# Moving some twenty entries of the order tables of an attention loop by one or two steps

## The chip, the cores and the metric

The kernel runs on one core of one Trainium2 chip. The metric is the device time of one execution in microseconds; the median of three runs is taken. Smaller is better.

## What is computed

The input x has 2048 tokens of 512 numbers in f32. Four residual layers follow one another, A, B, A, B, with the same weights for both A and both B. Each has 32 heads of 16.

```python
x = x + A(layernorm(x)); x = x + B(layernorm(x)); x = x + A(layernorm(x)); x = x + B(layernorm(x))
# A: linear attention, phi = concat(softmax(p), softmax(-p)) with p = head @ w_phi
kv, z = einsum(phi_k, v), sum(phi_k)
o = (phi_q @ kv) / (phi_q @ z + 1e-6)          # then o @ wo
# B: four segments s of 512 tokens, memory M, z carried from one to the next
a_dot = softmax(q_s k_s^T / 4 + causal mask) @ v_s
a_mem = (phi(q_s) @ M) / (phi(q_s) @ z + 1e-6)  # phi(t) = t + 1 or exp(t)
o_s = g * a_mem + (1 - g) * a_dot               # g = sigmoid(beta), then o @ wo
M, z = M + phi(k_s)^T v_s, z + sum(phi(k_s))
```

## The kernel before

**Order.** The program lists the instructions of every engine in the order in which they run. A helper chains each instruction to the one before it on its engine, so no engine takes a later one first: L208 records the matmuls, L212 the transposes on TensorE, and L186 everything on VectorE, ACT, GpSimd (POOL) and the DMA issues of SyncE (SP). That is why almost every row of the profile carries one of these three lines, and rows are told apart by the names of what they write and read. What an engine does next is therefore set by the tables below, and an instruction that waits holds everything behind it on its engine.

**Layer A** (`LayerA`, L653) has a first pass of feature steps for keys, values and queries, and a second pass for the products. In the first pass, run once at 33 to 174 us and once at 697 to 851 us, the table VALUES (L80) gives the step at which each of the quarters of the next segment's value projection is issued. Its first row is used once, for the first segment of the second A layer; the second row is used five times.

**Layer B** (`LayerB`, L1030) is run by `steps` (L1498), at 238 to 709 us and 915 to 1382 us. It has 160 steps, numbered k, 40 for each segment s; within a segment they are written m.j, with m from 0 to 7 (half of a group of eight heads) and j from 0 to 4. Each step does, in this order:

- `attend` (L1282): TensorE writes logits of scores into the PSUM tile lg (one buffer of two banks), ACT takes the exponential into P, POOL clears the masked half (affine_select);
- `maxima` (L1240), for the half nine steps ahead: TensorE writes logits into the tiles mx and my (one bank each), VectorE takes masked maxima from them into mxs, in two instructions of 128×512 or in four shorter ones;
- memory work that is due (POOL, SP, ACT), and then two lists of what was put off: `later` and `late`, with `weighted` (L1323, the product of P with v into the one bank pv, which ACT empties) between them; then the norm pieces that were put off as `rows`;
- the words of the table's cell for this step (`do`, L1510).

**The words.** q, k, v and out issue quarters of a projection or of the output, as many as stand behind the slash; a quarter is 6 matmuls on 64-row weights (tiles w, oh, ol) or 3 matmuls of 128×512 (wqk, hh, hl), and when a tile of 128 tokens is complete, its PSUM banks are emptied. These banks come from one pool, g, of three. A plus takes the next segment's projection. max is a transpose of the maxima into g, an ACT copy (mt) and a DMA. t0 to t3 are four transposes of one block of the keys' features into g and an ACT copy. x0 to x3 load a tile of the residual into xr (three buffers) with a DMA on SP, L1438. a and m read and update the memory, pre loads such a tile for the early part of the last output (tb), p its quarters, ln and n advance the normalization of a coming segment; an n is put into `rows`, so it runs in the next step, and depending on how far the norm is it issues a load of x on SP, or statistics, or an ACT normalization.

**The tilde.** Behind a word it sets `put_off` (L160, L163, L1511), and then the instruction that empties the last bank isn't issued in this step but appended to `late`:

```python
def wait(f):
    if put_off[0] is None:
        f()
    else:
        put_off[0].append(f)
```

For out that is the whole end of a tile (`end` in L1443): one addition on VectorE for each of its one or two PSUM banks, into xr, and the store of xr on SP. For a projection it is the subtraction on VectorE that leaves the low part.

**Tables.** FIRST (L86) orders segment 0, GAPS (L96) segments 1 and 2, LAST (L107) segment 3 of the first B layer and FINAL (L117) that of the second. BEFORE (L127) holds the steps ahead of k = 0. So an entry of GAPS is used four times, one of BEFORE twice, one of LAST or FINAL once.

Of the kernel before, what the change touches and what calls it, by code (L numbers as in the profile page):

```python
# [76 lines left out]
OUTROWS = ((), (1, 2, 3), (1, 2, 3), (1, 2, 3))  # L77
VROWS = ((3,), (0, 1, 2, 3), (0, 1, 2, 3), (0, 1, 2, 3))
ROWS = ((0, 2, 3, 4, 4, 8, 9, 11, 13), (4, 7, 9, 15))
VALUES = ((11, 12, 14, 15, 17, 19, 20, 22, 24, 25, 26, 27, 30, 32, 33, 35), (10, 11, 13, 14, 16, 18, 19, 21, 23, 24, 26, 27, 29, 31, 32, 34))  # L80
NORMS = (14, 20, 21, 21, 22, 23, 24, 27, 29, 31, 33)
OPENING = (0, 0, 1, 0, 1, 0, 1, 1, 1, 1, 0, 1, 1, 1, 1, 1, 1, 1, 1)

# [14 lines left out]
1.0 m0 n n q3/1 | 1.1 q3/2 | 1.2 n max q3/1~ | 1.3 t1 k3/2 | 1.4 k3/2~  # L98
2.1 max out/2 | 2.2 m1 | 2.3 ln ln out/1 | 2.4 a2 ln~ x0
3.1 max ln out/1~ | 3.2 x1 | 3.3 t2 q0+/4 | 3.4 out/3  # L100
4.0 out/1 x2 | 4.1 k0+/4~ max load | 4.3 out/2 | 4.4 n a3 out/2
5.0 t3 x3 m2 q1+/1 | 5.1 max q1+/2 | 5.2 q1+/1 | 5.3 out/2 n | 5.4 out/2
6.0 k1+/1 | 6.1 max k1+/3 | 6.2 m3 | 6.3 v0+/4 | 6.4 n a0+ v1+/2
7.0 n | 7.1 v1+/2 max begin | 7.2 n | 7.3 t0+ q2+/4~ n N | 7.4 v2+/4~ N
"""

LAST = """  # L107
0.1 max k2/4~ | 0.2 n | 0.3 v3/2 n | 0.4 a1 n v3/2~ n
1.0 n | 1.1 q3/3 max | 1.2 q3/1~ n | 1.3 k3/2 n | 1.4 k3/2~ n
2.1 max out/1 | 2.3 out/2 | 2.4 a2 x0 pre ln~  # L110
3.1 ln max ln~ | 3.3 x1 pre out/1 ln~ | 3.4 out/3
4.1 max | 4.2 out/1 | 4.3 pre out/3 x2 | 4.4 a3 out/1 v/2 x3
5.0 v/2 | 5.1 out/4 | 5.2 max | 5.3 fin v/2 | 5.4 v/2 pre
6.1 v/2 max | 6.3 v/2 fin | 6.4 v/2
7.1 pt v/2 p/3 | 7.2 v/2 | 7.3 fin v/2 p/3 | 7.4 p/3
"""
# [2 lines left out]
1.1 max q3/3 | 1.3 q3/1 | 1.4 k3/2  # L119
2.1 max k3/1 | 2.3 k3/1 out/1 pre | 2.4 a2 x0  # L120
3.1 max x1 out/2 | 3.3 out/1 pre | 3.4 out/2
4.1 out/2 | 4.2 max pre | 4.3 out/2 x2 | 4.4 a3 out/2
5.1 x3 out/2 | 5.2 max | 5.3 out/2 | 5.4 fin pre
6.1 max | 6.3 fin
7.0 pt | 7.1 p/2 | 7.3 p/3~ | 7.4 fin p/4
"""
BEFORE = {-25: 'v0 q0 load', -20: 'k0', -17: 'n', -16: 'n v1 n', -15: 'n n', -14: 'q1 n', -13: 'n', -12: 'k1 n n', -8: 'n v2', -6: 'q2~', -4: 't0', -3: 'max'}  # L127


@with_exitstack  # L130
def interleave_kernel(ctx, tc, x_in, a_wqkv, a_wphi, a_wo, b_wq, b_wk, b_wv, b_wo, b_beta,
# [416 lines left out]
    def v_tile(hT, w, vv, tag, order=range(4), paired=False, rows=()):  # L548

        v = sp.tile([P, 4, VROW], F32, tag="v", bufs=2, name=nm("v"))  # L550
        vv[:] = [v]
        if paired:
            for j in (0, 2 * VW - 1):
                pool.memset(v[:, :, 0 : H * VW].rearrange("p t (h e) -> p t h e", e=2 * VW)[:, :, :, j : j + 1], 1.0)
            pool.memset(v[:, :, H * VW : H * VW + 1], 1.0)
            shape = dict(e=2 * VW), slice(1, 2 * VW - 1), dict(e=2 * DH)
        else:
            pool.memset(v[:, :, 0 : H * VW].rearrange("p t (h e) -> p t h e", e=VW)[:, :, :, DH : DH + 1], 1.0)
            pool.memset(v[:, :, H * VW : VROW], 0.0)
            shape = dict(e=VW), slice(0, DH), dict(e=DH)  # L560
        for n, t in enumerate(order):
            vt = v[:, t, 0 : H * VW].rearrange("p (h e) -> p h e", **shape[0])[:, :, shape[1]]
            if n in rows:
                po = [PS(*tag) for _ in range(2)]
                yield from halves(po, lambda a, kc: hT[a][:, kc, t * P : (t + 1) * P], lambda b, kc: w[b][:, kc, :])
                act.copy(vt, po[0].rearrange("p (h e) -> p h e", **shape[2]))
                wait(lambda vt=vt, p=po[1]: dve.tensor_tensor(out=vt, in0=p.rearrange("p (h e) -> p h e", **shape[2]), in1=vt, op=ADD))
            else:
                po = PS(*tag)
                yield from tok_proj(po, hT, t, w)  # L570
                act.copy(vt, po.rearrange("p (h e) -> p h e", **shape[2]))
            yield
# [80 lines left out]
    class LayerA:  # L653
# [88 lines left out]
        def pass1(self, first):  # L742
# [35 lines left out]
            for n, s in enumerate(SEGS):  # L778
# [51 lines left out]
                if n < NSEG - 1:  # L830
                    hTs, g = upc
                    vv = []
                    plan = [(j, g) for j in ROWS[0 if n == 0 and not first else 1]]
                    vals, norms = VALUES[0 if n == 0 and not first else 1], NORMS
                    vt = v_tile(hTs, wv, vv, ("g", G))
# [194 lines left out]
    class LayerB:  # L1030
# [467 lines left out]
        def steps(self, side, after, table_end):  # L1498
# [71 lines left out]

            table = {k: (v.split(), 0) for k, v in BEFORE.items()}
            memory = {"a": {}, "m": {}}
# [122 lines left out]
```

## Time and profile before

| | |
|---|---|
| median of 3 runs | 1381.26 us (1380.68 to 1382.15) |
| profiled execution | 1383.75 us, its span 1382.0 us |
| granted TensorE clock | 0.998 |
| ACT: busy, instructions | 814.8 us, 1244 |
| GpSimd: busy, instructions | 735.5 us, 1073 |
| DMA | 225.35 MB, 163 GB/s on average |

A row of the timeline gives start and length in us, engine, line, operation, the tile written, the tiles read, shape, and how many such instructions follow in a row; in brackets stands how long the engine sat idle before it, and what ended this. A row of the waits gives engine, tile and line, what it waited for, and then the total, the number of times and the longest. Matmul lengths overlap, so what a matmul costs TensorE is read from the distance between starts. A row of the chain has start, length, engine or DMA, and tile.

### The profile page before, as it was taken

To read this page: it belongs to the slowest core of one execution; us is meant where nothing else is said; L and a number is where in the kernel's file an instruction comes from. 1 tells how busy PE (TensorE), PEld (TensorE's weight loads), DVE (VectorE), ACT (ScalarE), POOL (GpSimd) and SP (SyncE) were. 2 spreads that over 40 slices of the span, in tenths; PEclk is the share of its full clock that TensorE was granted. 3 is DMA by queue.
4 is the path that set the end of the run, shared out by engine and by line. 5 is a ranking of instruction groups with operands and counts; after the bars stand their busy time and mean duration, and the time that the engine had idled before them with its cause. 6 is when DMAs were issued, how large, how long until landed. Compare 5 with 4: busy or idle time off the path is not lost.

```text
span 1382.0 us, 34402 instructions
## 1 busy us (share of the span) xinstructions
PE 1353.2 (98%) x12598; PEld 962.1 (70%) x12598; DVE 986.8 (71%) x3074; ACT 814.8 (59%) x1244; POOL 735.5 (53%) x1073
## 2 busy tenths in 40 slices
PE   9999999999999999999999999999999999999998
PEld 8887878775666666665568887887656666666564
DVE  5766888587667667777547768958776776676774
ACT  5555445447686676666544434553676866866653
POOL 1678855224656666554534346642356656745543
PEclk9999999999999999999999999999999999999999
DMA  6369285546666647658541103855465666566552
GB/s 202 121 217 332 103 278 181 178 137 185 173 146 196 182 121 195 179 152 214 173 144 37 62 32 113 282 167 166 140 194 138 168 176 186 152 173 160 145 149 72
DMA packets 135735, 225.35 MB, mean 163 GB/s; under 512 B 21328, under 2 KB 39888, under 8 KB 135568
## 3 DMA queue, kind: packets, MB, share of 16 engines
q1 hardware_dynamic: 134464, 222.91, 55.7%
q8 instruction: 101, 1.65, 0.5%
q14 instruction: 66, 0.54, 0.1%
q10 hardware_dynamic: 1104, 0.24, 0.1%
HBM read 116.39 MB, written 43.25 MB: 116 GB/s over the span
## 4 chain that ended last, share of the span: by engine, by line
PE 84%; DVE 6%; DMA 3%; ACT 2%; issue 2%; POOL 2%; SPq 0%; POOLq 0%; DVEq 0%; ACTq 0%
PE g L208 51%; PE pv L208 11%; PE lg L208 8%; PE mx L208 5%; PE g L212 4%; PE my L208 3%; PE lg L212 2%; ACT P L186 1%; DVE junk L186 1%; PE pv L212 1%; DVE es L186 1%; POOL P L186 1%; DVE xr L186 1%; DVE ta L186 1%; DVE my L186 1%
## 5 line engine op out<-in xcount | busy, mean ns | idle before, releaser
L186 ACT ACTIVATE P<-lg 128x1024 f32<-128x1024 f32 x316 | 324.8, 1028 | 149.8 <-PE lg L208 128.4
L186 POOL TENSOR_SCALAR_AFFINE_SELECT P<-P 128x256 f32<-128x256 f32 (+1 forms) x448 | 190.6, 441 | 356.7 <-ACT P L186 350.2
L186 DVE CUSTOM_DVE_ANT_0 junk<-mx,mask 128x128 uint8<-128x128 f32 (+2 forms) x384 | 146.6, 420 | 88.5 <-PE my L208 54.4
L208 PE MATMUL g<-hh,wqk 128*128 128x512 f32 x512 | 187.3, 413 | 0.8 <-DMA wqk<-wqk 0.8
L208 PE MATMUL g<-w,oh 128*128 128x512 f32 (+1 forms) x652 | 172.9, 414 | 0.0
L208 PE MATMUL lg<-e,e 64*128 64x512 f32 (+1 forms) x1010 | 163.1, 373 | 4.7 <-ACT P L186 4.1
L208 PE MATMUL pv<-P,v 128*32 128x512 f32 (+3 forms) x2048 | 166.5, 441 | 0.1
L208 PE MATMUL g<-w,hh 64*128 64x512 f32 (+1 forms) x656 | 152.4, 407 | 2.9 <-ACT mmq L186 1.5
L208 PE MATMUL my<-e,e 63*128 63x256 f32 (+3 forms) x519 | 147.8, 345 | 4.8 <-DVE mxs L186 4.3
L208 PE MATMUL mx<-e,e 63*128 63x256 f32 (+3 forms) x519 | 147.6, 336 | 2.8 <-DVE mxs L186 2.8
L186 DVE CUSTOM_DVE_ANT_0 junk<-my,mask 128x128 uint8<-128x128 f32 (+2 forms) x384 | 146.9, 420 | 0.1
L208 PEld LDWEIGHTS lg<-e,e 64*128 64x128 f32 x1010 | 87.2, 185 | 84.2 <-issue 33.9
L186 DVE CUSTOM_DVE_ANT_0 mx<-mx,mask 128x512 f32<-128x512 f32 x128 | 89.0, 695 | 57.9 <-PE my L208 37.4
L208 PEld LDWEIGHTS pv<-P,v 128*32 128x32 f32 x2048 | 53.6, 109 | 101.2 <-issue 90.1
L208 PEld LDWEIGHTS g<-hh,wqk 128*128 128x128 f32 x512 | 96.3, 188 | 29.9 <-issue 9.2
L208 PEld LDWEIGHTS g<-w,oh 128*128 128x128 f32 (+1 forms) x652 | 93.8, 188 | 21.5 <-issue 9.1
L208 PE MATMUL g<-w,ol 128*128 128x512 f32 (+1 forms) x326 | 104.8, 396 | 1.6 <-DVE ol L186 1.6
L208 PEld LDWEIGHTS g<-w,hh 64*128 64x128 f32 (+1 forms) x656 | 89.5, 186 | 23.4 <-issue 4.3
L186 DVE DVE_READ_ACCUMULATOR2_ANT mxs<- 128x1 f32 x1024 | 101.0, 99 | 0.0
L208 PE MATMUL g<-hl,wqk 128*128 128x512 f32 x256 | 100.4, 392 | 0.0
L208 PEld LDWEIGHTS mx<-e,e 63*128 63x128 f32 (+1 forms) x519 | 91.7, 186 | 12.1 <-issue 4.5
L208 PEld LDWEIGHTS my<-e,e 63*128 63x128 f32 (+1 forms) x519 | 85.7, 186 | 17.7 <-DVE mxs L186 7.2
(191 smaller groups left out, 2897.3 us busy)
## 6 DMA issues: line engine op xcount, KB each, us to landing
e<-ta SPq DMA_DIRECT2D x384, 128.0 KB
wqk<-wqk SPq DMA_DIRECT2D x64, 512.0 KB
x<-x SPq DMA_DIRECT2D x48, 256.0 KB
xr<-x SPq DMA_DIRECT2D x32, 256.0 KB
x<-xr SPq DMA_DIRECT2D x28, 256.0 KB
tmp<-U SPq DMA_DIRECT2D x56, 128.0 KB
KN<-inv SPq DMA_DIRECT2D x28, 256.0 KB
pq<-tb SPq DMA_DIRECT2D x24, 256.0 KB
```

Of the source, the lines that this page charges most:

```text
L186: i = f(*a, **k)
L208: return held(nc.tensor.matmul(*a, **k))
L212: return held(nc.tensor.transpose(*a))
```

## The change

Only table entries move; no function changes and none is added or removed.

- VALUES, second row, sixth quarter: step 18 becomes 16.
- GAPS: of the two quarters of out in 4.4 one goes to 4.3; t3 goes from 5.0 to the end of 5.2; k1+ in 6.1 gets a tilde.
- LAST: in 1.1 max comes ahead of q3/3; the n of 1.3 goes to 1.2, as a second one there; the first ln goes from 3.1 to 3.0 (max then comes first in 3.1); pre goes from 4.3 to 5.0; v/2 leaves 4.4, so that the two quarters of 5.0 are now the first, and those behind it are issued in 5.1, ahead of out/4, which gets a tilde.
- FINAL: out/2 in 4.4 gets a tilde.
- BEFORE: the n of step −17 goes to step −15, as the third there.

```diff
-VALUES = (..., (10, 11, 13, 14, 16, 18, 19, 21, 23, 24, 26, 27, 29, 31, 32, 34))
+VALUES = (..., (10, 11, 13, 14, 16, 16, 19, 21, 23, 24, 26, 27, 29, 31, 32, 34))
 GAPS
-4.0 out/1 x2 | 4.1 k0+/4~ max load | 4.3 out/2 | 4.4 n a3 out/2
-5.0 t3 x3 m2 q1+/1 | 5.1 max q1+/2 | 5.2 q1+/1 | 5.3 out/2 n | 5.4 out/2
-6.0 k1+/1 | 6.1 max k1+/3 | 6.2 m3 | 6.3 v0+/4 | 6.4 n a0+ v1+/2
+4.0 out/1 x2 | 4.1 k0+/4~ max load | 4.3 out/3 | 4.4 n a3 out/1
+5.0 x3 m2 q1+/1 | 5.1 max q1+/2 | 5.2 q1+/1 t3 | 5.3 out/2 n | 5.4 out/2
+6.0 k1+/1 | 6.1 max k1+/3~ | 6.2 m3 | 6.3 v0+/4 | 6.4 n a0+ v1+/2
 LAST
-1.0 n | 1.1 q3/3 max | 1.2 q3/1~ n | 1.3 k3/2 n | 1.4 k3/2~ n
+1.0 n | 1.1 max q3/3 | 1.2 q3/1~ n n | 1.3 k3/2 | 1.4 k3/2~ n
 2.1 max out/1 | 2.3 out/2 | 2.4 a2 x0 pre ln~
-3.1 ln max ln~ | 3.3 x1 pre out/1 ln~ | 3.4 out/3
-4.1 max | 4.2 out/1 | 4.3 pre out/3 x2 | 4.4 a3 out/1 v/2 x3
-5.0 v/2 | 5.1 out/4 | 5.2 max | 5.3 fin v/2 | 5.4 v/2 pre
+3.0 ln | 3.1 max ln~ | 3.3 x1 pre out/1 ln~ | 3.4 out/3
+4.1 max | 4.2 out/1 | 4.3 out/3 x2 | 4.4 a3 out/1 x3
+5.0 pre v/2 | 5.1 v/2 out/4~ | 5.2 max | 5.3 fin v/2 | 5.4 v/2 pre
 FINAL
-4.1 out/2 | 4.2 max pre | 4.3 out/2 x2 | 4.4 a3 out/2
+4.1 out/2 | 4.2 max pre | 4.3 out/2 x2 | 4.4 a3 out/2~
-BEFORE = {-25: 'v0 q0 load', -20: 'k0', -17: 'n', -16: 'n v1 n', -15: 'n n', -14: 'q1 n', ...}
+BEFORE = {-25: 'v0 q0 load', -20: 'k0', -16: 'n v1 n', -15: 'n n n', -14: 'q1 n', ...}
```

More of the change, by code (lines that the diff above doesn't have):

```diff
@@ L79 @@
 ROWS = ((0, 2, 3, 4, 4, 8, 9, 11, 13), (4, 7, 9, 15))
-VALUES = ((11, 12, 14, 15, 17, 19, 20, 22, 24, 25, 26, 27, 30, 32, 33, 35), (10, 11, 13, 14, 16, 18, 19, 21, 23, 24, 26, 27, 29, 31, 32, 34))
+VALUES = ((11, 12, 14, 15, 17, 19, 20, 22, 24, 25, 26, 27, 30, 32, 33, 35), (10, 11, 13, 14, 16, 16, 19, 21, 23, 24, 26, 27, 29, 31, 32, 34))
 NORMS = (14, 20, 21, 21, 22, 23, 24, 27, 29, 31, 33)
@@ L126 @@
 """
-BEFORE = {-25: 'v0 q0 load', -20: 'k0', -17: 'n', -16: 'n v1 n', -15: 'n n', -14: 'q1 n', -13: 'n', -12: 'k1 n n', -8: 'n v2', -6: 'q2~', -4: 't0', -3: 'max'}
+BEFORE = {-25: 'v0 q0 load', -20: 'k0', -16: 'n v1 n', -15: 'n n n', -14: 'q1 n', -13: 'n', -12: 'k1 n n', -8: 'n v2', -6: 'q2~', -4: 't0', -3: 'max'}
 @with_exitstack
```

## The prediction

> **What bounds the kernel now.** I read the page first, for who is busy, and then the waits of TensorE.
>
> ```profile
> span 1382.0 us, 34402 instructions
> PE 1353.2 (98%) x12598; PEld 962.1 (70%) x12598; DVE 986.8 (71%) x3074; ACT 814.8 (59%) x1244; POOL 735.5 (53%) x1073
> ```
>
> TensorE sits idle for 1382.0 − 1353.2 = 28.8 us in all. The change alters no instruction, only the order, so those 28.8 us are the ceiling of what it can win. Where they lie by stage is told by the windows of the first and the second attention layer:
>
> ```profile
> 238.00:709.00 471.00, 462.50 (x3956) 304.69 (x3955) 324.65 (x1220) 299.02 (x437) 239.13 (x389) 1.00 0.61 168
> 915.00:1382.00 467.00, 455.02 (x3909) 298.94 (x3907) 322.71 (x1212) 290.12 (x425) 238.93 (x384) 0.99 0.57 156
> ```
>
> Idle there is 471.00 − 462.50 = 8.5 us and 467.00 − 455.02 = 12.0 us, so 20.5 of the 28.8 are in the loops that the tables order. The waits of TensorE say what ended them (total, times, longest):
>
> ```profile
> PE my L208 <- DVE mxs L186: 4.3, 18, 0.3
> PE mx L208 <- DVE mxs L186: 2.8, 3, 2.0
> PE g L208 <- ACT mmq L186: 1.5, 1, 1.5
> PE g L208 <- DVE e L186: 1.0, 1, 1.0
> ```
>
> The reader is to see two single waits of 2.0 and 1.5 us, one of 1.0, and a crowd of waits of about 0.3 in which the logits for the maxima (mx, my) find VectorE still reading the previous ones. An edit is worth something only where it puts TensorE's own work into one of these gaps, or makes the releaser come sooner. So I went from edit to edit and looked in the timelines for the gap beside it. The sum below is made against the profiled execution, 1383.75 us (its span 1382.0 and 1.75 around it), 2.5 us above the median of the runs, 1381.26; I carry the difference over unchanged.
>
> **FINAL 4.4, out/2 becomes out/2~ (second layer, once).** With "~", the two additions that empty the output's PSUM banks into xr, and the store behind them, run one step later, after that step's maxima.
>
> ```profile
> 1329.68 4.88 DMA xr<-x
> ```
> ```profile
> xr<-x SPq DMA_DIRECT2D x32, 256.0 KB
> ```
> ```profile
> 1332.76 0.40 PE L208 MATMUL my<-e,e 63*128 63x512 f32 x1
> 1334.30 0.51 PE L208 MATMUL lg<-e,e 64*128 64x512 f32 x2
> 1336.86 0.38 PE L208 MATMUL mx<-e,e 63*128 63x256 f32 x1 [2.05 <-DVE mxs L186]
> 1337.51 0.38 PE L208 MATMUL my<-e,e 63*128 63x256 f32 x1 [0.27 <-DVE mxs L186]
> 1342.86 0.56 PE L208 MATMUL lg<-e,e 64*128 64x256 f32 x4
> 1334.65 1.49 DVE L186 TENSOR_TENSOR xr<-g,xr 128x512 f32<-128x512 f32 x2 [2.80 <-DMA xr<-x]
> 1336.06 0.69 DVE L186 CUSTOM_DVE_ANT_0 mx<-mx,mask 128x512 f32<-128x512 f32 x1
> 1336.66 0.73 DVE L186 CUSTOM_DVE_ANT_0 my<-my,mask 128x512 f32<-128x512 f32 x1
> ```
>
> VectorE is free at 1334.65 − 2.80 = 1331.85, but first in its queue are the additions, which wait until 1334.65 for the load of x (4.88 us from its issue). Behind them stand the two maxima, whose logits have been there since 1332.76 + 0.40 = 1333.16, and TensorE stands behind these for 2.05 + 0.27 = 2.32 us. Moved, the maxima run from 1333.2 to 1333.2 + 0.69 + 0.73 = 1334.6, inside VectorE's idle 2.80; TensorE goes on with mx when its own logits end, at 1334.30 + 0.51 = 1334.8. The additions keep 1334.65 to 1336.14 (the load sets them), so the store's time does not change, but on SP the memory's loads of this half step (mmq, dn) go ahead of it and no longer queue behind it. What is late next: the following maxima can start on VectorE at 1336.14, where now the row of my ends at 1336.66 + 0.73 = 1337.4, and a second row group of the output waits for the first bank until about 1335.4. I take 2.5: the 2.32 of TensorE and a little of the next maxima, worked through to the logits at 1342.86, which then come near 1340.4. Ends: 0.8 (2.32 − 1.49, if the additions, now in the middle of the next step, delay that step by their whole length) and 3.1.
>
> [...]
>
> **GAPS 4.3 out/3, 4.4 out/1, and t3 from 5.0 to 5.2 (four uses: segments 1 and 2 of both layers).** One quarter of an output moves one step ahead, the four transposes of t3 two steps back; t3's ACT copy goes with them.
>
> ```profile
> 448.51 0.50 PE L208 MATMUL lg<-e,e 64*128 64x256 f32 x4 [0.63 <-ACT P L186]
> 452.01 1.28 PE L208 MATMUL pv<-P,v 128*32 128x512 f32 x16
> 453.53 0.66 PE L212 MATMUL g<-ident,tb 128*128 128x128 f32 x4
> 453.94 0.49 PE L208 MATMUL g<-hh,wqk 128*128 128x512 f32 x1
> 462.32 0.28 PE L208 MATMUL mx<-e,e 63*128 63x256 f32 x1
> 462.93 0.35 PE L208 MATMUL my<-e,e 63*128 63x256 f32 x1 [0.34 <-DVE mxs L186]
> 569.00 0.35 PE L208 MATMUL my<-e,e 63*128 63x256 f32 x1 [0.33 <-DVE mxs L186]
> 1139.82 0.35 PE L208 MATMUL my<-e,e 63*128 63x256 f32 x1 [0.34 <-DVE mxs L186]
> 451.27 0.69 ACT L186 ACTIVATE ot<-pv,bd 68x512 f32<-68x512 f32 x1 [1.19 <-POOL tmp L186]
> ```
>
> The quarter lands in front of the logits at 448.51, which wait 0.63 for the exponential on ACT: it fits there. But the product P·v at 452.01 needs the one pv bank, which ACT empties at 451.27 + 0.69 = 451.96 after POOL's chain, and that chain does not move. TensorE would come there 0.6 early and wait, so the quarter wins nothing in segment 1. The transposes hold TensorE for 453.94 − 453.53 = 0.41. At their new place, the step after next, my comes 462.93 − 462.32 = 0.61 after mx because VectorE still reads; TensorE reaches that point 0.41 sooner with the same VectorE, and spends the 0.41 on t3 in front of it or behind. I take 0.5 for each use, since the same wait stands at 569.00 in segment 2 and at 1139.82 in the second layer: 4 × 0.5 = 2.0. Ends: 0 (the next VectorE wait takes it back) and 4 × (0.63 + 0.61) = 5.0.
>
> **GAPS 6.1, k1+/3 becomes k1+/3~ (four uses).** A subtraction on VectorE goes behind the next maxima.
>
> ```profile
> 471.18 0.69 DVE L186 TENSOR_TENSOR ta<-g,ta 128x512 fp32r<-128x512 f32 x1 [1.44 <-ACT ta L186]
> 473.10 0.28 PE L208 MATMUL mx<-e,e 63*128 63x256 f32 x1
> 473.24 0.39 PE L208 MATMUL my<-e,e 63*128 63x256 f32 x1
> ```
>
> VectorE has been idle for 1.44 waiting for ACT, and the 0.69 then stands ahead of the maxima; my lags mx by 473.24 − 473.10 = 0.14 as a result. 4 × 0.14 = 0.6. Ends: 0.7 above, and below nothing, since the PSUM bank is held longer by up to two maxima; a rival, below.
>
> **VALUES, 18 to 16 (one quarter of the value projection earlier in the feature passes).**
>
> ```profile
> 126.10 0.72 PE L208 MATMUL g<-w,hh 128*128 128x512 f32 x2 [0.98 <-DVE e L186]
> 1331.74 0.72 PE L208 MATMUL g<-w,oh 64*128 64x512 f32 x4
> 1332.43 0.49 PE L208 MATMUL lg<-e,e 64*128 64x512 f32 x2
> ```
>
> A quarter holds TensorE for 1332.43 − 1331.74 = 0.69. Put ahead of the matmul at 126.10 it fills 0.69 of the 0.98 that this one waits for a bank. In the other uses TensorE waits for nothing there (the group "g <- DVE e" counts 1 wait in the whole run), so the quarter only changes places: 0. Sum 0.7; ends 0 and 1.0.
>
> **LAST (last segment of the first layer, once).** Three things count.
>
> ```profile
> 622.34 1.04 ACT L186 ACTIVATE P<-lg 128x1024 f32<-128x1024 f32 x1
> 623.24 0.83 ACT L186 ACTIVATE x<-x,st 128x512 f32<-128x512 f32 x1
> 623.75 0.50 PE L208 MATMUL lg<-e,e 64*128 64x512 f32 x2
> 636.48 0.50 PE L208 MATMUL lg<-e,e 64*128 64x512 f32 x2 [0.34 <-ACT P L186]
> 638.79 0.66 PE L212 MATMUL g<-ident,x 128*128 128x128 f32 x4 [0.74 <-ACT mt L186]
> 661.96 0.73 PE L208 MATMUL g<-w,hh 128*128 128x512 f32 x2 [1.52 <-ACT mmq L186]
> ```
>
> "n n" in one cell sends two normalizations of 0.83 to ACT ahead of the exponential at 622.34; that would start at 623.1 and end at 624.2, and the logits at 623.75, which write into what it reads, go to 624.2: a loss of 0.4 (ends 0.8 and 0). ln one step earlier fills the 0.34 ahead of the logits at 636.48 and takes something off the 0.74 at 638.79, but puts its VectorE work ahead of maxima: a gain of 0.1 (ends −0.2 and 1.1). v/2 leaves step 4.4, where it waits 1.52 for a bank that ACT empties after POOL's chain, and goes two steps back; TensorE does the next logits instead, and the pv bank, free shortly after the same ACT copies, takes a little of it: a gain of 1.4 (ends 0.3 and 1.5). The rest (max ahead of q3/3, the load pre behind x2, out/4~) I take at 0: TensorE does other matmuls over it, and it costs one SP issue, some 0.4, or one quarter, 0.69, where it doesn't. Sum 1.1; ends −0.6 and 2.6.
>
> **BEFORE, one n from −17 to −15 (both layers).** There the n only puts a load on SP's queue, two steps later. A step lasts 471.00/160 = 2.9 us, and a load of such a size 4.88; the norm's later n steps cover it. 0; without that cover up to 4.88 in each layer.
>
> **Sum:** 2.5 + 2.0 + 0.6 + 0.7 + 1.1 = 6.9 us. The profiled execution goes from 1383.75 to 1376.9 (span 1375.1), the median from 1381.26 to 1374.4.
>
> **The rivals.** *FINAL is given back.* The additions now fall in the middle of the next step, and the output of that step needs the banks which they empty; if TensorE waits there for as long as it did for the maxima, 2.5 fall away: 6.9 − 2.5 = 4.4, time 1376.9. For it: the additions end at 1336.14 either way. Against: three banks, and two maxima done meanwhile.
>
> *The small fills are absorbed.* As at 452.01, the next wait on a chain that does not move takes every small gain; what stays is FINAL's 2.5 and VALUES' 0.7: 3.2, time 1378.1. For it: segment 1's own quarter goes that way. Against: the maxima waits recur in every segment, with nothing behind them but TensorE's own pace.
>
> *The order is no bound.* If the idle slices only show where TensorE's backlog is read, and matmuls run slower where they are packed closer, the time stays: 1381.3. For it: 98% busy. Against: the two single waits are real stops, on a load and on POOL.
>
> *Slower: "~" holds the banks.* Each of the five larger "~" (FINAL one, k1+/3~ four) keeps a PSUM bank through two maxima, 0.69 + 0.73 = 1.4. With three banks and a group of matmuls every 0.69, the third group behind has to wait, at worst 5 × 1.4 = 7.0, while FINAL and k1 win nothing: 2.0 + 0.7 + 1.1 − 7.0 = −3.2, time 1384.5. It decides from a hold of 3.8/5 = 0.8 us each. For it: the wait at 126.10 is of this kind. Against: in all the waits on a bank that VectorE frees,
>
> ```profile
> PE g L208 <- DVE ol L186: 1.6, 2, 0.8
> ```
>
> that row and the one of 1.0 above are all there is, with two dozen "~" in the tables. [...]
>
> **How the numbers follow.** A measurement of this kernel can tell 0.2%, 2.8 us, from no change: faster means below 1378.5. The forecast has 0.60, FINAL given back 0.13, the small fills absorbed 0.13 (its 1378.1 is near the edge: 0.09 faster, 0.04 within), the order no bound 0.07, the banks 0.07. Faster 0.60 + 0.13 + 0.09 = 0.82, same 0.04 + 0.07 = 0.11, slower 0.07. For the range, the upper ends of the terms add up to 3.1 + 5.0 + 0.7 + 1.0 + 2.6 = 12.4, which would be 1368.9; they will not all come together, and I go a little over half of the way from 6.9, to 10.4: 1371.0. The other end takes in the absorbed fills with something lost in LAST: 1379.2. Left out are the order as no bound, the banks and a little at each end.
>
> **What would show it.** Right: the wait of mx for VectorE near 1337 is gone and the additions stand between two maxima; the 1.52 before v/2 is gone; the four waits of my at 5.x are below 0.2; TensorE idles about 22 us instead of 28.8. The normals show two in a row on ACT ahead of an exponential. Wrong: new waits "g <- DVE xr" or "g <- DVE ta" of 1 us and more (the banks), or P·v and logits that wait longer by what the maxima save (absorbed). My prediction fails if TensorE's idle time stays over 26 us.

## The result and the profile after

The changed kernel took 1374.73 us (median of 6 runs, 1373.16 to 1376.23) beside 1381.97 for the kernel before (6 runs): ratio 0.9949, interval 0.9936 to 0.9961, or 7.0 us less. Timed again later (below) it gave 0.9969 (0.9957 to 0.9981), 4.3 us less. Both are inside the range, and their middle, 5.7, is nearer to what the stages show than the first figure.

The profile's page and the waits of TensorE in the profiled execution of the changed kernel:

```profile
span 1374.5 us, 34392 instructions
PE 1349.6 (98%) x12598; PEld 960.7 (70%) x12598; DVE 987.9 (72%) x3074; ACT 813.2 (59%) x1244; POOL 734.1 (53%) x1073
```
```profile
PE my L208 <- DVE mxs L186: 2.7, 13, 0.3
PE mx L208 <- DVE mxs L186: 2.3, 2, 1.7
PE pv L208 <- ACT ot L186: 1.7, 3, 0.7
...
PE g L208 <- DVE e L186: 0.3, 1, 0.3
```

TensorE idles 1374.5 − 1349.6 = 24.9 us, 3.9 less than the 28.8 of before, under the 26 that the prediction named as its failure but not down to its 22, while the span is 7.5 shorter. So almost half of the difference between these two profiles isn't idle time but TensorE being busy for a shorter time (1353.2 to 1349.6) with the same 12598 matmuls. The prediction took the 28.8 for the ceiling of what the change can win, as if the busy time were fixed, so the first question is where this comes from. Of the single waits, the 1.0 for e is down to 0.3 and the 1.5 for mmq is gone, but the longest wait of mx is still 1.7, at another place; P·v now waits 1.7 for ot: 0.69 and 0.70 in segment 1 of the two layers, which is the absorption that was forecast at 452.01, and 0.35 in LAST.

FINAL's place, first the starts of the logits of steps 143 and 150 before, then in the changed kernel:

```profile
1327.04 0.39 PE L208 MATMUL lg<-e,e 64*128 64x256 f32 x2
...
1346.53 0.50 PE L208 MATMUL lg<-e,e 64*128 64x512 f32 x2
```
```profile
1323.93 0.39 PE L208 MATMUL lg<-e,e 64*128 64x256 f32 x2
...
1334.45 0.47 PE L208 MATMUL my<-e,e 63*128 63x512 f32 x1 [0.22 <-DVE mxs L186]
...
1339.94 0.50 PE L208 MATMUL lg<-e,e 64*128 64x512 f32 x2
```
```profile
1330.00 0.70 DVE L186 CUSTOM_DVE_ANT_0 mx<-mx,mask 128x512 f32<-128x512 f32 x1 [1.26 <-PE mx L208]
...
1330.62 0.73 DVE L186 CUSTOM_DVE_ANT_0 my<-my,mask 128x512 f32<-128x512 f32 x1
...
1331.52 1.42 DVE L186 TENSOR_TENSOR xr<-g,xr 128x512 f32<-128x512 f32 x2
```

The maxima stand ahead of the additions, and the waits of 2.05 and 0.27 are gone; one of 0.22 is new a step later, where VectorE now has the additions behind it. The seven steps went from 19.49 to 16.01, 3.5 less, more than the 2.32 of the waits. The granted clock, the third figure from the end in the windows of the profile of before, points to the rest:

```profile
1334.00:1343.00 9.00, 6.69 (x55) 4.24 (x49) 6.14 (x19) 2.80 (x5) 4.13 (x6) 0.81 0.36 102
...
1348.00:1351.00 3.00, 2.93 (x19) 1.06 (x19) 1.92 (x8) 0.16 (x1) 0.41 (x1) 0.61 0.98 282
```

Elsewhere in the loops it is 1.00; looked at in windows of 1 us, two stretches of about 3.4 us run at 0.5, the first from 1338.4, shortly behind the stall, the second from 1348.6. The profile of the changed kernel has none. Four matmuls of oh on 64 rows hold TensorE for 0.86 inside the first stretch (1338.54 to 1339.40) and for 0.46 ahead of the stall (1328.86 to 1329.32). If all of its work takes about twice as long at half the clock, that is 1.7 us for each stretch, an estimate, and 3.4 in all: nearly the 3.6 by which its busy time fell. The busy times alone don't prove it, since in the profiles below without a stretch in the loops they lie between 1348.5 and 1351.2. Whether the stall had brought this on, or chance, had to be found out.

### The profile page after: what moved, and what is told of

It reads as the page before. It is cut to its first block, busy times and chain, and to the rows that moved or that the text cites. A ratio compares the mean times of both kernels' runs of the same rounds, so it can differ in the third digit from the quotient of the medians.

```text
span 1374.5 us, 34392 instructions
## 1 busy us (share of the span) xinstructions
PE 1349.6 (98%) x12598; PEld 960.7 (70%) x12598; DVE 987.9 (72%) x3074; ACT 813.2 (59%) x1244; POOL 734.1 (53%) x1073
## 4 chain that ended last, share of the span: by engine, by line
PE 84%; DVE 6%; DMA 4%; ACT 2%; POOL 1%; issue 1%; SPq 0%; ACTq 0%; POOLq 0%; DVEq 0%
PE g L208 50%; PE pv L208 10%; PE lg L208 8%; PE mx L208 5%; PE g L212 4%; PE my L208 3%; PE lg L212 2%; DMA wqk<-wqk 1%; DVE junk L186 1%; ACT P L186 1%; DMA xr<-x 1%; DVE es L186 1%; PE pv L212 1%; POOL P L186 1%; DVE xr L186 1%
```

## The stages in all profiles

All tables below go by the distance between the starts of the first logits of two steps, as in the rows above, since a local distance is much steadier than a whole run: where nothing was edited, steps 31 to 60 take 75.03 to 75.20 in fourteen profiles. Times in us:

| stage (steps) | edits absent | edits present |
|---|---|---|
| GAPS, segment 1 (60 to 80) | 55.71 to 55.81 | 55.17 to 55.26 |
| GAPS, segment 2 (100 to 120) | 54.53 to 54.61 | 53.76 to 53.88 |
| LAST, second n (128 to 133) | 10.53 to 10.58 | 10.90 to 10.92 |
| LAST, ln (133 to 140) | 17.26 to 17.30 | 16.65 to 16.69 |
| LAST, v/2 (143 to 150) | 22.76 to 24.64, mean 23.6 without ln | 22.59 to 24.48, mean 23.4; alone 21.76 |
| FINAL (143 to 150, second layer) | 16.39 to 19.50 | 15.71 to 16.00 |

The row of segment 1 leaves out one use of twelve: in a profile with the edits, the second layer's took 55.86. The first four rows repeat to about 0.1. The last two do not, edited or not: there a DMA ends the wait, and its arrival differs from run to run: VectorE waits 1.57 to 2.80 for xr in four profiles that keep FINAL's stall (before, LAST alone, VALUES alone, and the change without the tilde), and 0.37 to 2.24 for dm in five with all of LAST, or all but the second n.

## Experiments: the four parts alone

```diff
 FINAL (alone: f1)
-4.3 out/2 x2 | 4.4 a3 out/2
+4.3 out/2 x2 | 4.4 a3 out/2~
```

> Before, with the tilde of FINAL 4.4 alone. Two theories of what that edit is worth. Stall alone: TensorE's waits of 2.05 and 0.27 us near 1337 go and nothing else, so 2.3 to 2.5 us. Stall and clock: in the profile of before the granted clock is 0.5 from about 1338.3 to 1341.6 and from about 1348.6 to 1352, after the stall, and 1.00 everywhere in the profile of after; if the stall brings these on, the edit wins 2.4 for the stall and up to 3.3 for the two stretches, in all 4 to 5 us, and the clock is 1.00 to the end. If the stretches come by chance, they stay or come back here, and the edit is worth 1 to 2.5.

Measured: 1378.61 us, ratio 0.9993 (0.9983 to 1.0003), 1.0 us less, and so neither the 2.3 of the stall alone nor the 4 of stall and clock. Steps 143 to 150 take 15.75, and the clock is 1.00 to the last output. The next three kernels are the kernel before with the edits of one table each (the diff is that of the change).

> Before, with the three edits of GAPS alone. By the prediction 2.6 us in four places, about 0.55 in each segment 1 and 0.7 in each segment 2 by the starts of the steps in the trace of after. If the next waits absorb them, under 1. FINAL's stall is still here: if it brings on the low clock, a stretch at 0.5 follows it in this profile too; if that is chance, in some of these profiles there is none.

Measured: 1377.64, ratio 0.9987 (0.9976 to 0.9999), 1.8 less.

> Before, with the edits of LAST alone. Predicted 1.1: minus 0.4 for the two normals ahead of an exponential, 0.1 for ln, 1.4 for v/2. The starts of the steps in the trace of after give minus 0.4, plus 0.5 and about plus 0.1 to 0.3, in all 0.3 to 0.5, with a new wait of mx for VectorE of about 1.7 in place of the old 1.52: VectorE stands behind the load of xr in both. So this theory says no difference that can be measured, the prediction minus 1.1. FINAL's stall is still here, so a low clock after it is expected where the stall brings it on.

Measured: 1379.39, ratio 0.9997 (0.9985 to 1.0009).

> Before, with the edits of VALUES and BEFORE alone. Predicted 0.7 for the one wait of 0.98 in the first A layer, and 0 for BEFORE; the trace of after has 0.65 there, and about 0.1 in each of three other uses, so 0.7 to 1.0. If the matmul behind it waits for the same bank anyway, 0. FINAL's stall is still here.

Measured: 1379.53, ratio 0.9995 (0.9985 to 1.0006). All four are under 1 and small; only GAPS is clear of no difference by its time alone. What they show best is FINAL's stall, which three of them keep. The row in which mx waits, in GAPS alone, LAST alone, and VALUES alone:

```profile
1331.45 0.38 PE L208 MATMUL mx<-e,e 63*128 63x256 f32 x1 [0.43 <-DVE mxs L186]
```
```profile
1333.80 0.38 PE L208 MATMUL mx<-e,e 63*128 63x256 f32 x1 [1.28 <-DVE mxs L186]
```
```profile
1334.68 0.39 PE L208 MATMUL mx<-e,e 63*128 63x256 f32 x1 [0.82 <-DVE mxs L186]
```

The same instruction, with the same code around it, waits 0.43, 1.28, 0.82, and 2.05 in the profile on which the prediction stood. No low stretch followed in these three: the granted clock is 1.00 in every us up to 1374. So the 2.5 of the prediction was read from the longest of these waits.

## Experiments: the whole, its undoing, and the load

Four kernels on one chip. The first is the changed kernel unchanged; the second is it without FINAL's tilde; the third undoes the second n:

```diff
 LAST, in the changed kernel (n1)
-1.2 q3/1~ n n | 1.3 k3/2 |
+1.2 q3/1~ n | 1.3 k3/2 n |
 FINAL, in the kernel before (x2_early)
-4.1 out/2 | 4.2 max pre | 4.3 out/2 x2 |
+4.1 out/2 x2 | 4.2 max pre | 4.3 out/2 |
```

> The changed kernel as it is, timed again on one chip beside the kernels below. The four parts alone gave 0.9 for FINAL, 1.8 for GAPS, 0.4 for LAST and 0.7 for VALUES by their ratios, 3.8 us in all; the starts of the steps in their traces give 0.9, 2.5, 0.4 and 0.7, so 4.5. If the parts add up and the first profile of before was an unlucky one, this comes out at 3.5 to 5. If the parts need one another, it stays at 7.

Measured: 1375.75, ratio 0.9969 (0.9957 to 0.9981), 4.3 less: the parts add up (3.8 by their times), and nothing in the stages says that they need one another.

> The changed kernel without the tilde of FINAL 4.4. In the profiles that keep this stall, mx waited 2.05 (before), 0.43, 1.28 and 0.82 (three parts alone), as the load of x took longer or shorter; the mean is 1.15, and my's 0.27 comes on top. So the tilde is worth about 0.9 in most executions: this comes out 0.5 to 1.5 slower than the changed kernel, with a clock of 1.00 there. By the prediction it is 2.5 slower; by stall and clock 4.

Measured: 1376.21, ratio 0.9972 (0.9964 to 0.9981): 0.4 slower than the changed kernel, inside the intervals of both. Its profile has the wait again, 1.16, and 17.16 for the stage, against 15.71 in the run of the changed kernel beside it.

> The changed kernel with the second n of LAST 1.2 back in 1.3. By the prediction this edit lost 0.4 (a second normalization of 0.83 ahead of an exponential), and the starts of the steps show minus 0.37 at that place in two traces. If what it loses stays lost, this is 0.4 faster than the changed kernel; if the waits for DMAs later in LAST take it back, the same. Either way the logits of that step no longer come late.

Measured: 1374.26, ratio 0.9957 (0.9946 to 0.9969), the fastest of all kernels on that chip; 1.5 less than the changed kernel beside it, with intervals that overlap. The stage itself is clear: 10.58 in place of 10.90. In the changed kernel the two normalizations stand as one row of two on ACT ahead of the exponential, and the logits behind it wait:

```profile
619.53 1.52 ACT L186 ACTIVATE x<-x,st 128x512 f32<-128x512 f32 x2
620.94 1.03 ACT L186 ACTIVATE P<-lg 128x1024 f32<-128x1024 f32 x1
```
```profile
622.02 0.50 PE L208 MATMUL lg<-e,e 64*128 64x512 f32 x2 [0.28 <-ACT P L186]
```

So one edit of the change did lose its 0.35, as forecast, and nothing gave it back.

> Before, with x2 of FINAL asked for in 4.1 in place of 4.3, ahead of pre, and no tilde. If it is the load that keeps VectorE's additions and with them the maxima, the wait of mx for VectorE near 1335 goes just as with the tilde, and the gain is about 0.9, as for the tilde alone. If the additions keep the maxima by their own 1.49, or the earlier load waits for an xr buffer on SP and holds up what is behind it there, a wait of 0.4 or more stays or a new one comes up.

Measured: 1379.71, ratio 0.9997 (0.9985 to 1.0008). The time tells nothing at this size; the profile does. The additions now wait for TensorE and not for the load, mx no longer waits, and my keeps its 0.27:

```profile
1333.30 1.49 DVE L186 TENSOR_TENSOR xr<-g,xr 128x512 f32<-128x512 f32 x2 [0.79 <-PE g L208]
```
```profile
1336.15 0.39 PE L208 MATMUL my<-e,e 63*128 63x256 f32 x1 [0.27 <-DVE mxs L186]
```

The stage takes 16.01 without any tilde. What kept mx was the load in front of the additions; their own length leaves the 0.27 of my.

## Experiments: parts of parts, and a longer stall

```diff
 t3_and_v: in GAPS only t3 moved; in LAST only
-4.3 pre out/3 x2 | 4.4 a3 out/1 v/2 x3 / 5.0 v/2 | 5.1 out/4
+4.3 out/3 x2 | 4.4 a3 out/1 x3 / 5.0 pre v/2 | 5.1 v/2 out/4~
```

> Before, with t3 of GAPS moved and with v/2, pre and out/4~ of LAST moved, which lie in different stages and are read from the starts of the steps. In GAPS: if t3 alone fills the gap at my, each of segments 1 and 2 comes out 0.41 to 0.44 shorter than before (steps 60 to 80 take 55.76 before, steps 100 to 120 take 54.56); if it needs the quarter, less. In LAST, steps 143 to 150 took 22.8 to 24.5 without the edits of LAST (mean 23.8) and 22.6 to 24.5 with them (mean 23.4): predicted was 1.4 shorter, so 22.4; if the loads set this stage, it lies anywhere from 22.6 to 24.5, and the wait of 1.52 for mmq is replaced by one of mx for VectorE.

Measured: segment 1 took 55.29 and 55.32 in the two layers, segment 2 54.21 and 54.16, so t3 alone wins 0.45 and 0.38. In LAST the stage took 21.76, the shortest seen, in one profile; with all of LAST it was 22.59 to 24.48. This kernel and the next were executed once each, 1376.81 and 1382.75 us, which is too few to compare their times.

> Before, with the quarter of GAPS moved from 4.4 to 4.3 and with ln of LAST moved to 3.0. By the prediction the quarter wins nothing in segment 1 (55.76 for steps 60 to 80, P times v takes it back) and about 0.16 in segment 2 (54.40 for steps 100 to 120). ln was predicted at 0.1; in the traces with all of LAST, steps 133 to 140 took 16.68 where they take 17.28 without, so 0.60 is expected if ln is the cause.

Measured: segment 1 took 55.79 and 55.81, no gain; segment 2 54.37 and 54.35, 0.2 less. P·v waits for ACT as it does in the changed kernel; the row is from this run:

```profile
451.58 1.28 PE L208 MATMUL pv<-P,v 128*32 128x512 f32 x16 [0.71 <-ACT ot L186]
```

ln alone shortens steps 133 to 140 from 17.28 to 16.65, by 0.63. Here a stretch at 0.50, from 1337.9 to 1341.4, followed FINAL's wait of 1.23.

```diff
 ln_later, in the changed kernel with the second n undone
-3.3 x1 pre out/1 ln~ | ... | 4.2 out/1 |
+3.3 x1 pre out/1 | ... | 4.2 out/1 ln~ |
```

> The changed kernel with the second n back in 1.3 and, besides, the last ln of LAST moved from 3.3 to 4.2, so that its two loads of the next layer's weights are issued behind the stack of step 140 on SP and not ahead of it. If these loads hold up what VectorE waits for in steps 143 to 150, this stage comes down from 22.6 to 24.5 to 22 or less and the wait of mx for VectorE there goes; the kernel is then 0.4 for n and about 1 faster than the changed one. If the loads don't matter, the stage stays, and if v/2 then waits for its weights, it gets longer.

Measured: 1376.00, ratio 0.9974 (0.9962 to 0.9985), no gain on the changed kernel, and the stage took 24.96. Yet the wait at which the edit aimed is gone: dm, a small load of the memory that VectorE awaits ahead of the maxima of step 144, is there in time, and mx waits for nothing in that step. The next load behind the moved ones on SP, that of xr, is late instead:

```profile
653.51 0.54 DVE L186 RECIPROCAL dm<-dm 128x64 f32<-128x64 f32 x1
...
660.52 1.49 DVE L186 TENSOR_TENSOR xr<-g,xr 128x512 f32<-128x512 f32 x2 [2.66 <-DMA xr<-x]
```

In the five other profiles with all of LAST, or all but the second n, VectorE waits 0.37 to 2.24 for dm. So the two loads of weights may well have held dm up, and moving them shifted the wait to xr; one profile can't settle it. The new wait of mx behind this was followed by a low stretch:

```profile
662.73 0.38 PE L208 MATMUL mx<-e,e 63*128 63x256 f32 x1 [1.00 <-DVE mxs L186]
```
```profile
660.00:663.00 3.00, 2.00 (x9) 1.10 (x7) 2.37 (x5) 1.02 (x1) 1.58 (x4) 1.00 0.04 16
664.00:667.00 3.00, 3.00 (x8) 1.96 (x10) 1.41 (x8) 0.15 (x1) 0.43 (x1) 0.50 0.77 258
```

The last kernel makes FINAL's stall longer.

```diff
 FINAL, in the kernel before (x2_late)
-4.3 out/2 x2 | 4.4 a3 out/2
+4.3 out/2 | 4.4 a3 x2 out/2
```

> Before, with x2 of FINAL asked for in 4.4 in place of 4.3, behind the memory's loads of that step on SP, so about 1.6 later: a longer dose of the stall. If the stall's price is its length, mx waits 1.15 and 1.6, about 2.8, and the kernel is about 1.6 slower than before. If a stall of 2 us or more also brings the clock down, a stretch at 0.5 of some 3.4 us follows in this profile and the mean clock is below 1.000 in most runs, and it is 3 or more slower. If the low stretches come by chance, the share of runs below 1.000 is as in before (15 of 35).

Measured: 1382.14, ratio 1.0018 (1.0010 to 1.0027), 2.5 slower. In its profile mx waits 1.68, longer than the 1.07 on average of the seven profiles that keep the stall as it was but not the 2.8 expected, and the windows behind it show the clock:

```profile
1335.20 0.38 PE L208 MATMUL mx<-e,e 63*128 63x256 f32 x1 [1.68 <-DVE mxs L186]
```
```profile
1331.00:1335.00 4.00, 2.52 (x26) 1.03 (x22) 1.90 (x3) 2.84 (x4) 1.96 (x3) 1.00 0.18 63
1336.00:1339.00 3.00, 3.00 (x16) 3.00 (x18) 1.47 (x8) 0.00 (x0) 0.50 (x1) 0.50 0.56 137
1340.00:1344.00 4.00, 4.00 (x45) 2.76 (x37) 3.89 (x14) 2.69 (x5) 1.53 (x4) 1.00 0.07 19
```

Every run comes with its mean clock, rounded to a thousandth; one stretch of 3.4 us at half speed takes 1.7/1380, so it shows as 0.999. The mean also counts the end, where TensorE has nothing left to do: the profile of LAST alone has 0.999 for a stretch that starts 2.0 us behind its last matmul and costs TensorE nothing. Below 1.000 were 11 of 11 runs of this kernel; of the kernel before, 32 of 82 on the three chips; of the four kernels with other edits and this stall (GAPS, LAST, VALUES alone, and the change without the tilde), 23 of 48; of the five in which the tilde or the early load removes it (f1, both timings of the changed kernel, n1, x2_early), 7 of 40. A sixth kernel with the tilde, ln_later, has 9 of 12, but a stall of its own. So the shares speak for it that the stall brings the low clock on, the more surely the longer it lasts, and that a rest comes without it: the changed kernel's second profile has a stretch from 1339.1 to 1342.5 behind waits of 0.34 and 0.19 only, and 1.74 in LAST of its first profile was followed by none. The stretches that lie inside the loops are alike in height and length: 0.50 for 3.4 us, twice in before, and once in x2_late, quarter_and_ln, ln_later and the second profile of the changed kernel. In before the second begins 10.2 us behind the first. Ahead of the four that followed a stall mx had waited 1.00 to 2.05. In the 3.4 us ahead of a stretch TensorE idled 2.14 (before), 1.95 (x2_late), 1.50 (quarter_and_ln) and 1.26 us (ln_later), but only 0.66 ahead of the second stretch of before and 0.65 ahead of that in the changed kernel. How much is enough, and what else decides, stays open.

## Why the prediction was right, and where its terms were not

The time, 1374.4 forecast, and the direction came out; the terms by the stages:

| term | forecast | by the stages |
|---|---|---|
| FINAL | 2.5 | 1.0 at full clock, 3.3 with a low stretch |
| GAPS, quarter and t3 | 2.0 | 0.45 + 0 and 0.4 + 0.2, twice: 2.1 |
| GAPS, tilde | 0.6 | not run alone; the rest of 2 × (0.55 + 0.73) = 2.56: 0.5 |
| VALUES | 0.7 | 0.6, and 0.13 in three other uses: 1.0 |
| LAST | 1.1 | −0.35 + 0.62 + about 0.2 on average (1.0 where dm is in time) = 0.5 |
| BEFORE | 0 | no difference shows |

*FINAL.* The mechanism was right in the main: the maxima ran in VectorE's gap, the load no longer kept them, and no wait for a bank came. Two points were not. The additions did not keep the load's time: in all five profiles with the tilde they start right behind the maxima and wait for no load. And "a little of the next maxima" is a loss: in the step behind, my starts 0.63 behind mx in place of 0.11 and waits the 0.22 seen above, and this step takes 2.73 to 2.75 with the tilde where it takes 2.22 or 2.23 with the stall at a full clock. So the rival in which FINAL is given back came in part, 0.5, through VectorE; no wait for xr or a bank stands in its stage.

The size was wrong too. The profiles that keep the stall and a full clock take 16.39, 17.26, 16.82, 17.16 and 16.52 for the stage (mean 16.83), those with the tilde 15.75, 16.00, 15.71, 15.76 and 15.73 (mean 15.79): 1.0. What varies is the wait of mx: without it the first five would take 15.96 to 16.00, and x2_early, which has none, takes 16.01. Measured against this the stage is 1.4 to 1.5 longer in the three profiles with a low stretch in it (before, x2_late, quarter_and_ln, 18.67 to 19.50), so that is what a stretch costs here. With the mean of all seven waits, 1.07, the tilde is worth 1.3 at a full clock. The step that failed is "I take 2.5: the 2.32 of TensorE and a little of the next maxima": a wait that ends on a DMA was taken from one execution as if it were the program's. The forecast named a low end of 0.8, because the additions might delay the next step, and the truth lies near that. In the first profile of before the stall happened to be long and two low stretches followed, one of them in this stage, so that pair of profiles shows more for FINAL, 3.5, than the prediction had.

*GAPS* is right to a tenth in both terms: the quarter was absorbed in segment 1 by P·v and won 0.2 in segment 2, t3 filled the gap at my (0.45 and 0.38), the tilde won about 0.1 a use. The rows that showed it in the changed kernel are these, where mx and my now start without a wait:

```profile
461.61 0.28 PE L208 MATMUL mx<-e,e 63*128 63x256 f32 x1
461.79 0.38 PE L208 MATMUL mx<-e,e 63*128 63x256 f32 x1
461.81 0.44 PE L208 MATMUL my<-e,e 63*128 63x256 f32 x2
```

*VALUES.* The matmul at 126.10 now waits 0.28 in place of 0.98, as worked out:

```profile
125.98 0.73 PE L208 MATMUL g<-w,hh 128*128 128x512 f32 x2 [0.28 <-DVE e L186]
```

The distance of four steps around it fell from a mean of 6.44 (eight profiles, 6.26 to 6.62) to 5.85 (six, 5.66 to 6.10). That the other uses win nothing was wrong by 0.13 each in three of them (7.42 to 7.29 for four steps in one). No idle time of TensorE shows there, so what gives the 0.13 stays open. BEFORE's n, forecast at 0, ran only together with VALUES; from the last projections of the first pass to step 31 the kernels without the two take 220.7 to 223.1 us in the two layers and those with them 221.1 to 223.3, so no difference shows.

*LAST.* The loss of the second n was right (0.4 forecast, 0.35). ln was undersized, 0.1 for 0.62: its transposes didn't only fill the 0.34, the step behind it lost its wait on mt, the 0.74, too, and got one of 0.52 for VectorE: 0.34 + 0.74 − 0.52 = 0.56. v/2 looks oversized, 1.4 for about 0.2, but its mechanism came out: the wait of 1.52 for mmq went (0.84 to 1.49 in the six other profiles without the edit), and P·v waits 0.26 to 0.36 for ot in the five profiles with ln and v/2 moved, the "little" that the pv bank was to take. What hides the gain is the load dm. In the changed kernel it came late and mx waits 1.74 for the maxima behind it; in before mx waits 0.41 at the same place. TensorE's row, and VectorE's in the changed kernel and in before:

```profile
656.76 0.35 PE L208 MATMUL mx<-e,e 63*128 63x256 f32 x1 [1.74 <-DVE mxs L186]
```
```profile
655.43 0.55 DVE L186 RECIPROCAL dm<-dm 128x64 f32<-128x64 f32 x1 [2.24 <-DMA dm<-den]
```
```profile
656.39 0.55 DVE L186 RECIPROCAL dm<-dm 128x64 f32<-128x64 f32 x1 [0.91 <-DMA dm<-den]
```

Its wait differs from run to run: up to 0.91 in the six profiles without ln and v/2, 1.15 with ln alone, 0.37 to 2.24 in those five. Three profiles have no wait for dm and the same steps ahead of it: the stage takes 21.76 with v/2 moved (t3_and_v), 22.76 and 22.81 without (x2_early, x2_late). So v/2 wins 1.0 when the load comes alike, and what LAST loses again belongs to dm. The step that failed is that the gains of ln and v/2 were added as if no load stood behind them: with ln earlier, VectorE comes about 0.6 sooner to a load that arrives at its own time. That the longer waits come from this is likely and not shown, and what fixes the arrival stays open; ln_later points to the two loads of weights ahead of it.

The sum by the stages is 1.0 + 2.1 + 0.5 + 1.0 + 0.5 = 5.1 at full clock, and a little more for the low stretches that come less often: 18% of the runs instead of about 40%, at 1.5 each 0.3, an estimate that also counts stretches at the end. The two timings of 7.0 and 4.3 lie on either side. So the forecast of 6.9 held because its range was wide enough for a term that was too large by 1.5; that the first timing met it to 0.3 us is luck.

## What to carry to other kernels

Two waits that end on another engine's work in program order came back here to a few hundredths (0.33 or 0.34 for my, 0.94 to 0.98 for e) and could be priced from one profile; the wait of mx, which hangs on a DMA, was one draw of many (0.43 to 2.05), and such a wait wants several profiles before it is priced. When an edit removes such a wait, look at what else on the same engine waits for DMAs of the same stage, for that came late next here (2.66 for xr, once dm was in time), and compare profiles in which that load came alike: the means hid 1.0 for v/2. Local distances between two instructions of a profile settled here what whole runs, that scatter by several us (1376.86 to 1383.80 for the kernel before on one chip), could not.

## What the chip showed that was not expected

A stop of TensorE of 1.0 to 2.05 us can cost a second time: in the profiles of x2_late, ln_later, of before and of quarter_and_ln it was followed by about 3.4 us at a granted clock of 0.5, which lengthened the stage by 1.4 to 1.5 us where that can be told, while stops of 1.28, 1.16 and 1.74 in other profiles were not. All 11 runs of the kernel with the lengthened stall had a mean clock below 1.000, and 7 of 40 of the five kernels without it.
